# Long convolution and two MLPs on one core: sums move from GpSimd to VectorE, the filter's clamps are shared with ScalarE, the last rows go from SBUF to SBUF

## The chip, the cores and the metric

The kernel runs on one core of one Trainium2 chip. The metric is device time in microseconds (us): the median of the runs of one program. In this text PE is TensorE, PEld its weight loads, DVE is VectorE, ACT is ScalarE, POOL is GpSimd and SP is SyncE; ACTq and SPq are the DMA queues of ACT and SP.

## What is computed

```python
h_filt = (np.maximum(pos_emb @ w1, 0.0) @ w2) * np.exp(-0.01 * pos)[:, None]
u = x * v                                            # 12480 x 128
y = irfft(rfft(u, n=2 * S, axis=0) * rfft(h_filt, n=2 * S, axis=0), n=2 * S, axis=0)[:S]
a = x * y                                            # convolution, then the gate
b = np.maximum(a @ moe_w_in, 0.0) ** 2 @ moe_w_out        # 128 -> 2048 -> 128
g = b @ moe2_w_in
out = g * (1.0 / (1.0 + np.exp(-1.702 * g))) @ moe2_w_out # 128 -> 2048 -> 128
```

The MLP weights are 64-bit floats in memory; the kernel splits each into two 32-bit parts.

## The kernel before

The order of the work is written out by hand: each engine takes its instructions in the order in which the code issues them, and so do the two DMA queues. There are four stages.

**Filter stage** (`filter_stage`). Eight groups of eight columns j. For each, PE multiplies eight position tiles by `w1` (L256, `hp`), DVE clamps and windows the two halves of the result into `r` (L261, two instructions of 512 elements), and the sum and the difference of the halves go to `h`: the sum on POOL (L265; on DVE in the last group), the difference on DVE (L267). `spare` (L246) issues matmuls whose results nobody reads, 5 ahead of the stage and 13 behind it. A matmul of 32-bit floats shows as two records.

**First transform** (`s1_step`, L278, L282): the 16 steps of the filter `h`, then the 32 of the input `u`, into `G` and `A`.

**Second transform** (`stage_s2`): 99 frequencies, in 50 pairs p. Per pair PE makes `xk` (L348), now and then `fk` (L325) and `hk` (L340) for the filter, and with two pairs' delay the way back `ob` (L369). DVE multiplies (`t`, L357), and the two halves of the product are made on POOL (L360) and DVE (L361). ACT copies `ob` into `A` (L371; one PSUM buffer for `ob`), and every second pair the rows go to the DRAM tile `bd` (L378). `work.tick(p)` puts one step of the weights' conversion behind each pair's product: a chunk of 512 columns is eight DVE instructions (L135 to L148, L152) and one ACT cast (L150), one step to a tick; seven chunks start 6.5 pairs apart.

**Handover**. The last three rows go to `bd` (L374), then `load_first` (L458) reads rows 88 to 98 back into `A`, transposed; `work.finish()` completes two chunks; `sums_first` (L433) makes six sums on DVE; `front_y(0)` runs the inverse transform (L516, `yps`) of the first tile, `split_first` (L504 to L506) multiplies by x, and the MLP starts. `spare` (L645) issues 8 matmuls ahead of it and one behind it.

**MLP** (`mlp`). 25 tiles of 490 to 504 columns, each in 8 units per layer. `unit_in` (L560 to L562, L578, `hin`) is the first product of a unit with ACT's ReLU and square (L588, L589) or sigmoid (L593); `gate` and `low` (L601, L603, L612) make the two parts `gh` and `gl`; `unit_out` (`acc`) follows four units later. The first 40 units belong to layer 0; from then on layers 0 and 1 alternate. For the next tile `load_b` fetches 198 KB pieces `uv` from `bd` and POOL makes four sums `b` of 256 elements out of each (L433); `front_y` does the inverse transform and the product with x (L529; the columns that are left over, `yr`, on POOL, L532). Eight more weight chunks of 512 columns are converted, one step to a unit, started 6 units apart.

Of the kernel before, what the change touches and what calls it, by code (L numbers as in the profile page):

```python
# [1 line left out]

# [21 lines left out]
N1, N2 = 99, 127  # L24
# [7 lines left out]
NWC = DFF // WC  # L32
NP = -(-N1 // 2)
# [16 lines left out]
LAG = 4  # L50
SHIFT = 40
# [18 lines left out]
def widths():  # L70

    whole = [sum(s[3] for s in WHOLE[SPT * t:SPT * t + SPT]) for t in range(NTILE)]
    rest, left = [], RESTW
    for t, w in enumerate(whole):
        n = 0
        if t and left:
            n = min(left, -(-RESTW // (NTILE - 1)))
# [18 lines left out]
def conv_mlp_kernel(ctx: ExitStack, tc: tile.TileContext, xc, xt, vc, pt, w1, w2,  # L96
# [16 lines left out]
    def load_raw(n, pool):  # L113
        i, c = divmod(n, NWC)
        raw = pool.tile([128, WC, 2], I32, tag="raw", name="raw", bufs=2)
# [3 lines left out]
        else:  # L119
            k = WC // 128  # L120
# [4 lines left out]
    def conversion(n, raw, pool):  # L125

        i, c = divmod(n, NWC)
        cols = slice(c * WC, (c + 1) * WC)  # L130
        low, high = raw[:, :, 0], raw[:, :, 1]
        s = pool.tile([128, WC], I32, tag="cs", name="cs", bufs=2)
        hi, lo = (wts[i // 2][:, 2 * (i % 2) + k, cols] for k in range(2))
        vec = nc.vector
        yield vec.tensor_scalar(out=s, in0=high, scalar1=20, scalar2=0x7FF,  # L135
                                op0=ALU.logical_shift_right, op1=ALU.bitwise_and)
        yield vec.tensor_scalar(out=s, in0=s, scalar1=896.0, scalar2=1151.0, op0=ALU.max, op1=ALU.min)
        yield vec.tensor_scalar(out=s, in0=s, scalar1=896.0, scalar2=float(1 << 23),
                                op0=ALU.subtract, op1=ALU.mult)
        yield vec.scalar_tensor_tensor(out=s, in0=high, scalar=-(1 << 31), in1=s,  # L140
                                       op0=ALU.bitwise_and, op1=ALU.bitwise_or)
        m = pool.tile([128, WC], I32, tag="cm", name="cm", bufs=2)
        f = m.bitcast(FP32)
        yield vec.tensor_scalar(out=m, in0=high, scalar1=0xFFFFF, scalar2=0x100000,
                                op0=ALU.bitwise_and, op1=ALU.bitwise_or)
        yield vec.scalar_tensor_tensor(out=f, in0=low.bitcast(U32), scalar=2.0 ** -32, in1=m,
                                       op0=ALU.mult, op1=ALU.add)
# [11 lines left out]
    class Weights:  # L159
# [3 lines left out]
        def __init__(self, chunks, start, gap, lead, pool, rest=()):  # L163
            self.pool, self.raw, self.run = pool, {}, []
            self.plan = [(int(start + k * gap), n) for k, n in enumerate(chunks)]
            self.fetches = [(at - lead, n) for at, n in self.plan] + [(at, n) for at, n in rest]
            self.plan += [(1 << 30, n) for at, n in rest]

        def tick(self, i):
            self.run = [g for g in self.run if next(g, self) is not self]  # L170
            if self.fetches and self.fetches[0][0] <= i:
                n = self.fetches.pop(0)[1]
                self.raw[n] = load_raw(n, self.pool)
            if self.plan and self.plan[0][0] <= i and self.plan[0][1] in self.raw:
                n = self.plan.pop(0)[1]
                self.run.append(conversion(n, self.raw.pop(n), self.pool))
                next(self.run[-1])

        def finish(self):
            while self.run or self.plan:  # L180
                self.tick(1 << 30)

# [37 lines left out]
    def filter_stage(fp, bank, h, inputs):  # L220
# [4 lines left out]
        warm = fp.tile([128, 128], FP32, name="warm", bufs=1)  # L225
# [22 lines left out]
        spare(5, warm[:, 1:128], warm[:, 1:128])  # L248
        for j in range(0, NJ, JF):
            for c in range(j // HC + 12, min(j // HC + 12 + JF // HC, NC_)):  # L250
                load_pos(c)
            if j >= JF:
                inputs.load()
            ps = bank("hp")[:N1]
            for i in range(JF):
# [8 lines left out]
            last = j + JF == NJ  # L264
            (nc.vector if last else nc.gpsimd).tensor_tensor(  # L265
                out=h[:, :, j:j + JF], in0=r[:, 0], in1=r[:, 1], op=ALU.add)
            nc.vector.tensor_tensor(out=h[:, :, NJ + j:NJ + j + JF], in0=r[:, 0], in1=r[:, 1],  # L267
                                    op=ALU.subtract)
        spare(13, p_t[NC_ - 1][:, 0, :], bw1)
# [35 lines left out]
    def stage_s2(sp, mp, A, w2b, hooks, work):  # L305
# [9 lines left out]
        with kp as kp, obp as obp:  # L315
# [49 lines left out]
            def back(p):  # L365
                n, m, P = pair(p), m_t.pop(p), P_t.pop(p)
                ob = obp.tile([128, 2, 2, D], FP32, tag="ob", name="ob")
# [3 lines left out]
                nc.scalar.copy(out=A[:, 2 * p:2 * p + n], in_=ob[:, 0:n])  # L371
                if p == NP - 1:
                    for h, queue in ((0, nc.scalar), (1, nc.sync)):
                        queue.dma_start(out=bd[h, 0:JF1, k], in_=A[h * NJ:h * NJ + JF1, k])  # L374
# [6 lines left out]
            for p in range(NP + 2):  # L381
# [6 lines left out]
                elif p % 4 == 0:  # L388
                    filters(p // 2)
                    filters(p // 2 + 1)  # L390
                if 0 <= p - 2:
# [6 lines left out]
                if p < NP - 2:  # L398
# [7 lines left out]
    def tile_parts(segs):  # L406

        at = 0
# [7 lines left out]
    b_t, x_t = {}, {}  # L416
# [14 lines left out]
    def combine(k, s, c, engine):  # L431
        uv, b = b_t[k]
        engine.tensor_tensor(out=b[:, :, s, c], in0=uv[:, 0, :, c], in1=uv[:, 1, :, 1 - c],  # L433
                             op=ALU.add if s != c else ALU.subtract)

    def load_b(bp, t):


        last = max(p[0] for p in whole(t)) // JG
        for k in range(loaded[0], last + 1):  # L440
            uv = bp.tile([N1, 2, JG, 2, D], FP32, tag="uv", name="uv", bufs=2)
            for h in range(2):
                nc.sync.dma_start(out=uv[:, h], in_=bd[h, k * JG:(k + 1) * JG].rearrange("j k c d -> k j c d"))
            b = sums(bp, (k - 1) % 3)
            b_t[k] = uv, b
            for s in range(1 if k < KF else 2):
                for c in range(2):
                    combine(k, s, c, nc.gpsimd)
        loaded[0] = last + 1

    late_h = []

    def load_first(A, rows):


        for h in range(2):
            queue = nc.scalar if rows.stop == N1 and h else nc.sync
            queue.dma_start(out=A[rows, h * JF1:(h + 1) * JF1],  # L458
                            in_=bd[h, 0:JF1, rows].rearrange("j k c d -> k j c d"))
        for h, k in late_h:  # L460
            nc.sync.dma_start(out=bd[h, JF1:NJ, k], in_=A[h * NJ + JF1:(h + 1) * NJ, k])
# [387 lines left out]
```

## Time and profile before

| | |
|---|---|
| median of 3 runs (lowest, highest) | 1390.95 us (1390.25, 1391.91) |
| the profiled execution: its own time, its span | 1392.53 us, 1390.7 us |
| busy: PE, PEld | 1377.2 us (99%), 1143.1 us (82%) |
| busy: DVE, ACT, POOL | 1104.7 us (79%), 949.6 us (68%), 208.9 us (15%) |
| granted TensorE clock, mean | 0.998 |
| HBM read, written | 63.62 MB, 24.81 MB |

The profiled execution's own time is 1.83 us more than its span: what lies ahead of the first and behind the last instruction. Busy shares are of the whole span. The filter stage takes about the first 22 us, the transforms last until 227 us, the handover until 239 us, and the MLP takes the rest; what the change touches lies mostly at the seams, so it is read there and not in the shares.

### The profile page before, as it was taken

Reading aid. Unit: us, or ns where it says so; the run is one execution under the profiler, and the core shown is the slowest. Engines: PE = TensorE matmul, PEld = TensorE weight load, DVE = VectorE, ACT = ScalarE, POOL = GpSimd, SP = SyncE. Lnnn points to the kernel's source line nnn. Section 1 sums busy time; section 2 is a strip of 40 time slices with the busy share of each in tenths; the row PEclk is TensorE's granted clock in tenths of the full one; section 3 lists DMA queues with packets and bytes.
Section 4 is the critical chain, followed back from the end, with each engine's and each line's share of the span. In section 5 each row is a group of like instructions: output and inputs, shape, how many; then the busy total and the mean of one; then the engine's idle time right before and its main releaser. Section 6 shows DMA issues by size and latency. Waiting matters only on the chain.

```text
span 1390.7 us, 19236 instructions
## 1 busy us (share of the span) xinstructions
PE 1377.2 (99%) x7756; PEld 1143.1 (82%) x7756; DVE 1104.7 (79%) x1170; ACT 949.6 (68%) x1071; POOL 208.9 (15%) x208
## 2 busy tenths in 40 slices
PE   9999998999999999999999999999999999999998
PEld 8888885878788888888888888888888888888887
DVE  7559997888997777778777877777777777778887
ACT  2655553888776776667677776777677766777776
POOL 3013333522221011201121011111110120000000
PEclk9999999999999999999999999999999999999999
DMA  9967785212100001000010000100000100000000
GB/s 261 307 215 265 269 266 178 77 50 69 47 20 27 25 10 32 27 27 9 20 39 27 8 27 20 39 9 27 20 27 8 39 19 9 8 8 8 8 15 15
DMA packets 46583, 89.67 MB, mean 64 GB/s; under 512 B 4221, under 2 KB 31038, under 8 KB 45982
## 3 DMA queue, kind: packets, MB, share of 16 engines
q1 hardware_dynamic: 37427, 63.69, 15.1%
q10 hardware_dynamic: 9067, 24.75, 4.7%
q8 instruction: 61, 1.00, 0.3%
q14 instruction: 28, 0.23, 0.0%
HBM read 63.62 MB, written 24.81 MB: 64 GB/s over the span
## 4 chain that ended last, share of the span: by engine, by line
PE 79%; DVE 2%; ACT 2%; issue 0%; ACTq 0%
PE acc L560 13%; PE hin L560 13%; PE hin L561 13%; PE acc L561 13%; PE hin L562 12%; PE acc L562 12%; PE yps L516 3%; DVE gl L612 1%; ACT g L589 1%; ACT g L588 1%; DVE gh L601 0%; DVE g L603 0%; ACT gh L591 0%; DVE lo L493 0%; PE hin L578 0%
## 5 line engine op out<-in xcount | busy, mean ns | idle before, releaser
L612 DVE TENSOR_TENSOR gl<-g,gh 128x1004 fp32r<-128x1004 f32 (+4 forms) x400 | 493.6, 1234 | 33.8 <-ACT gh L608 33.6
L588 ACT ACTIVATE g<-hin 128x1004 f32<-128x1004 f32 (+4 forms) x200 | 201.1, 1005 | 226.9 <-PE hin L562 214.5
L560 PE MATMUL acc<-gh,w 128*128 128x502 f32 (+4 forms) x800 | 314.0, 392 | 2.4 <-DVE lo L493 2.4
L561 PE MATMUL acc<-gl,w 128*128 128x502 f32 (+4 forms) x800 | 312.1, 390 | 1.3 <-DVE gl L612 1.2
L562 PE MATMUL acc<-gh,w 128*128 128x502 f32 (+4 forms) x800 | 311.6, 390 | 0.0
L560 PE MATMUL hin<-hi,w 128*128 128x502 f32 (+4 forms) x798 | 311.3, 390 | 0.3 <-DVE g L603 0.3
L561 PE MATMUL hin<-lo,w 128*128 128x502 f32 (+4 forms) x798 | 311.0, 390 | 0.0
L562 PE MATMUL hin<-hi,w 128*128 128x502 f32 (+4 forms) x798 | 310.5, 389 | 0.0
L603 DVE TENSOR_TENSOR g<-hin,g 128x1004 f32<-128x1004 f32 (+4 forms) x200 | 238.6, 1193 | 46.6 <-ACT g L593 46.4
L601 DVE CAST gh<-g 128x1004 fp32r<-128x1004 f32 (+4 forms) x185 | 132.8, 718 | 152.0 <-ACT g L589 152.0
L593 ACT ACTIVATE g<-hin 128x1004 f32<-128x1004 f32 (+4 forms) x200 | 200.0, 1000 | 73.8 <-PE hin L562 65.8
L589 ACT ACTIVATE g<-g 128x1004 f32<-128x1004 f32 (+4 forms) x200 | 208.0, 1040 | 6.3
L608 ACT CAST gh<-g 128x1004 fp32r<-128x1004 f32 (+4 forms) x200 | 202.7, 1014 | 1.7 <-DVE g L603 1.7
L560 PEld LDWEIGHTS acc<-gh,w 128*128 128x128 f32 x800 | 150.9, 189 | 35.6 <-DVE lo L493 2.8
L560 PEld LDWEIGHTS hin<-hi,w 128*128 128x128 f32 x798 | 150.5, 189 | 34.8 <-ACT g L588 2.1
L561 PEld LDWEIGHTS acc<-gl,w 128*128 128x128 f32 x800 | 150.7, 188 | 31.9 <-DVE gl L612 2.5
L562 PEld LDWEIGHTS acc<-gh,w 128*128 128x128 f32 x800 | 150.7, 188 | 30.7
L562 PEld LDWEIGHTS hin<-hi,w 128*128 128x128 f32 x798 | 150.8, 189 | 30.4
L561 PEld LDWEIGHTS hin<-lo,w 128*128 128x128 f32 x798 | 150.9, 189 | 29.9
L433 POOL TENSOR_TENSOR Gs<-uv 99x256 f32<-99x256 f32 x82 | 91.8, 1149 | 442.2 <-DMA uv<-bd 367.2
L433 POOL TENSOR_TENSOR b<-uv 99x256 f32<-99x256 f32 x44 | 48.9, 1140 | 269.9 <-DMA uv<-bd 194.8
L360 POOL TENSOR_TENSOR P<-t 128x256 f32<-128x256 f32 (+1 forms) x50 | 48.1, 961 | 155.6 <-DVE t L357 139.2
(72 smaller groups left out, 1047.2 us busy)
## 6 DMA issues: line engine op xcount, KB each, us to landing
uv<-bd SPq DMA_DIRECT2D x64, 198.0 KB
m<-in_c_s_dram SPq DMA_DIRECT2D x49, 256.0 KB
bd<-A ACTq DMA_DIRECT2D x24, 512.0 KB
x<-in_xc_dram SPq DMA_DIRECT2D x16, 384.0 KB
v<-in_vc_dram SPq DMA_DIRECT2D x16, 384.0 KB
Gs<-gd ACTq DMA_DIRECT2D x10, 512.0 KB
raw<-in_moe_w_in_dram SPq DMA_DIRECT2D x8, 512.0 KB
raw<-in_moe_w_out_dram SPq DMA_DIRECT2D x8, 512.0 KB
```

What stands on the lines that cost most here:

```text
L360: nc.gpsimd.tensor_tensor(out=P[:, 0:n, 1], in0=t[:, 0:n, 0, 1], in1=t[:, 0:n, 1, 0], op=ALU.add)
L433: engine.tensor_tensor(out=b[:, :, s, c], in0=uv[:, 0, :, c], in1=uv[:, 1, :, 1 - c], op=ALU.add if s != c else ALU.subtract)
L560: nc.tensor.matmul(out=out, lhsT=a, rhs=hl[0], start=first, stop=False)
L561: nc.tensor.matmul(out=out, lhsT=a, rhs=hl[1], start=False, stop=False)
L562: nc.tensor.matmul(out=out, lhsT=b, rhs=hl[0], start=False, stop=last)
L588: nc.scalar.activation(out=g, in_=ps, func=ACTF.Relu)
L589: nc.scalar.activation(out=g, in_=g, func=ACTF.Square)
L593: nc.scalar.activation(out=g, in_=ps, func=ACTF.Sigmoid, scale=1.702)
L601: nc.vector.tensor_copy(out=gh, in_=g)
L603: nc.vector.tensor_tensor(out=g, in0=ps, in1=g, op=ALU.mult)
L608: nc.scalar.copy(out=gh, in_=g)
L612: nc.vector.tensor_tensor(out=gl, in0=g, in1=gh.bitcast(FP32), op=ALU.subtract)
```

## The change

- Filter stage: `r` is laid out column by column (j outside, f inside) with three buffers. ACT clamps half of the second half, a quarter of the layer, in four instructions of 64 elements each (L287), except in the last group, which is cut into two groups of four columns. The sum and the difference are therefore written to `h` with one element every 128 words. 7 spare matmuls stand ahead of the stage (5 before) and 6 behind it (13 before).
- Second transform: all eight layer-0 chunks are ticked there, started exactly 6 pairs apart, and the ticks end four pairs before the last instead of two; the last filter group is made two pairs earlier; the next to last `ob` takes another PSUM buffer, the last one is copied by DVE.
- Handover: rows 92 to 98 go straight from SBUF to SBUF, one row and half to a DMA (L402), rows 88 to 91 through `bd` as before. Three ticks of the conversion run ahead of the first sums, the rest of it behind the first tile's front. That front is cut in pieces with small spares between them.
- MLP: POOL's sums go to DVE, two instructions of 512 elements for a piece instead of four of 256, one of them issued ahead of each layer-0 gate (`combine_next`). Pieces are fetched a tile earlier. Layer 1's weights are converted in four chunks of 1024 columns, 12 units apart, in one shared tile `words`. The left-over columns' product goes to DVE, and left-over columns start in tile 2 instead of 1.

```diff
-            r = fp.tile([N1, 2, F, JF], FP32, tag="r", name="r")
-            for s in range(2):
-                wb = win[:, s, j:j + JF].unsqueeze(1).to_broadcast([N1, F, JF])
-                nc.vector.scalar_tensor_tensor(
-                    out=r[:, s], in0=ps.rearrange("p (j s f) -> p s f j", j=JF, s=2)[:, s],
-                    scalar=0.0, in1=wb, op0=ALU.max, op1=ALU.mult)
...
+            ps = ps.rearrange("p (j s f) -> p s j f", j=JF, s=2)
+            late = j + JF >= NJ
+            r = fp.tile([128, 2, JF, F], FP32, tag="r", name="r", bufs=3)[:N1]
+            for s, n in ((0, m), (1, m if late else HC)):
+                wb = win[:, s, j:j + n].unsqueeze(2).to_broadcast([N1, n, F])
+                nc.vector.scalar_tensor_tensor(out=r[:, s, 0:n], in0=ps[:, s, 0:n], scalar=0.0, in1=wb,
+                                               op0=ALU.max, op1=ALU.mult)
+            if not late:
+                for i in range(HC, m):
+                    nc.scalar.activation(out=r[:, 1, i], in_=ps[:, 1, i], func=ACTF.Relu,
+                                         scale=win[:, 1, j + i:j + i + 1])
+            for n, (engine, op) in enumerate(((nc.vector if late else nc.gpsimd, ALU.add),
+                                              (nc.vector, ALU.subtract))):
+                engine.tensor_tensor(out=h[:, :, n * NJ + j:n * NJ + j + m].rearrange("p f j -> p j f"),
+                                     in0=r[:, 0, 0:m], in1=r[:, 1, 0:m], op=op)
+        spare(6, p_t[NC_ - 1][:, 0, :], bw1)
...
+                ob = (kp.tile([128, FK, D], FP32, tag="fk", name="ob", bufs=1).rearrange(
+                    "p (k c) d -> p k c d", c=2) if p == NP - 2 else
+                      obp.tile([128, 2, 2, D], FP32, tag="ob", name="ob"))
...
+                (nc.vector.tensor_copy if p == NP - 1 else nc.scalar.copy)(
+                    out=A[:, 2 * p:2 * p + n], in_=ob[:, 0:n])
+                for i in range(2 * p, 2 * p + n):
+                    if i >= DIRECT:
+                        for h, queue in ((0, nc.scalar), (1, nc.sync)):
+                            queue.dma_start(out=A[i:i + 1, h * JF1:(h + 1) * JF1],
+                                            in_=A[h * NJ:h * NJ + JF1, i])
+                if p == NP - 4:
+                    load_first(A, slice(88, DIRECT))
...
-                if p < NP - 2:
+                if p < NP - 4:
                     work.tick(p)
...
+    def combine_two(uv, b, op):
+        b = b.rearrange("n j s c d -> n j (s c) d")
+        u, v = uv[:, 0], uv[:, 1]
+        if op == ALU.add:
+            nc.vector.tensor_tensor(out=b[:, :, 1:3], in0=u[:, :, ::-1], in1=v, op=op)
+        else:
+            nc.vector.tensor_tensor(out=b[:, :, 0:4:3], in0=u, in1=v[:, :, ::-1], op=op)
+    def combine_next(n):
+        for i in range(min(n, len(pending))):
+            pending.pop(0)()
...
+            for a, b, n in ((0, 2, 2), (2, 3, 4), (3, SPT, 0)):
+                at = inverse(ps, whole(0)[a:b], at)
+                if n:
+                    spare(n, 128)
...
-        spare(8)
+        spare(4)
         front_y(0)
         spare(1)
-        load_rest()
+        load_b(bp, 1)
+        combine_next(2)
+        work.finish()
         prev = None
-        work = Weights([8, 12, 9, 13, 10, 14, 11, 15], 3, 6, 3, cp)
+        work = Weights([(2, 0), (3, 0), (2, 1), (3, 1)], 6, 12, 4)
...
+                if l == 0:
+                    combine_next(1)
                 gate(un)
...
-            work = Weights([0, 4, 1, 5, 2, 6, 3], 3, 6.5, 5, cp, [(46, 7)])
+            work = Weights([(i, c) for c in range(NWC) for i in range(2)], 3, 6, 5)
...
-            load_first(A, slice(88, N1))
-            work.finish()
+            store_late(A)
+            work.finish(EARLY)
             sums_first(bp, A)
```

`DIRECT` is 92, `EARLY` 3 and `NP` 50. `store_late` writes the last row's columns to `bd` on SP.

**DVE, filter stage, one group and the last one.** `r<-hp` are the clamps, `h<-r` the difference (and, in the last group, the sum). Before:

```order
L261 SCALAR_TENSOR_TENSOR r<-hp,win 99x512 x2
L267 TENSOR_TENSOR h<-r 99x64x8
L261 SCALAR_TENSOR_TENSOR r<-hp,win 99x512 x2
L265 TENSOR_TENSOR h<-r 99x64x8
L267 TENSOR_TENSOR h<-r 99x64x8
```

Now:

```order
L283 SCALAR_TENSOR_TENSOR r<-hp,win 99x512
L283 SCALAR_TENSOR_TENSOR r<-hp,win 99x256
L291 TENSOR_TENSOR h<-r 99x8x64
L283 SCALAR_TENSOR_TENSOR r<-hp,win 99x256 x2
L291 TENSOR_TENSOR h<-r 99x4x64 x2
L283 SCALAR_TENSOR_TENSOR r<-hp,win 99x256 x2
L291 TENSOR_TENSOR h<-r 99x4x64 x2
```

One clamp of each group is half as long, the result is written with f inside, and the last group has two of everything.

**DVE, from the last products to the first sums** (`t` and `P` are the product of a pair, `cs`, `cm`, `words` and `w` the conversion, `Gs<-A` the six first sums). Before:

```order
L357 TENSOR_TENSOR t<-xk,hc 128x512
L361 TENSOR_TENSOR P<-t 128x128
L148 SCALAR_TENSOR_TENSOR cm<-cm,cs 128x512
L135 TENSOR_SCALAR cs<-raw 128x512
L137 TENSOR_SCALAR cs<-cs 128x512
L138 TENSOR_SCALAR cs<-cs 128x512
L152 TENSOR_TENSOR w_958<-cm,w_958 128x512
L140 SCALAR_TENSOR_TENSOR cs<-raw,cs 128x512
L144 TENSOR_SCALAR cm<-raw 128x512
L146 SCALAR_TENSOR_TENSOR cm<-raw,cm 128x512
L433 TENSOR_TENSOR Gs<-A 99x2x128 x6
```

(of which `L148` and `L152` come once more ahead of `L433`). Now:

```order
L381 TENSOR_TENSOR t<-xk,hc 128x512
L385 TENSOR_TENSOR P<-t 128x128
L397 COPY A<-ob 128x256
L153 SCALAR_TENSOR_TENSOR words<-words 128x512
L157 TENSOR_SCALAR words<-words 128x512
L171 TENSOR_TENSOR w_987<-words,w_987 128x512
L159 TENSOR_SCALAR words<-words 128x512
L465 TENSOR_TENSOR Gs<-A 99x2x128 x6
```

Ten conversion instructions stood there, four are left, and the copy of the last row is new; the others follow the first tile's front.

**ACT, at the same place, now** (`A<-A` are row DMAs, `w_987<-words` the last two casts of the conversion, `g` the first units' ReLU and square):

```order
L397 COPY A<-ob 128x512
L402 DMA A<-A 1x4x256 x3
L169 CAST w_987<-words 128x512 x2
L653 ACTIVATE g<-hin 128x2x492
L654 ACTIVATE g<-g 128x2x492
```

The second cast stands ahead of the first unit's ReLU; before, both casts were ahead of the first sums.

## Rows read from the trace of the kernel before

**Rows 1.** The page's first part: busy us, share of the span, instructions.
```profile
PE 1377.2 (99%) x7756; PEld 1143.1 (82%) x7756; DVE 1104.7 (79%) x1170; ACT 949.6 (68%) x1071; POOL 208.9 (15%) x208
```
**Rows 2.** Waits of PE, whole span: us in total, times, longest.
```profile
PE acc L560 <- DVE lo L493: 2.4, 1, 2.4
...
PE acc L561 <- DVE gl L612: 1.2, 2, 0.7
```
**Rows 3.** Three stretches: length, busy PE, PEld, DVE, ACT, POOL, clock, DMA share, GB/s.
```profile
160.00:200.00 40.00, 40.00 (x295) 34.78 (x295) 38.44 (x48) 20.20 (x32) 13.65 (x15) 1.00 0.81 267
230.00:243.00 13.00, 11.10 (x63) 6.45 (x62) 8.17 (x15) 1.84 (x3) 4.44 (x6) 0.87 0.63 193
350.00:400.00 50.00, 47.60 (x234) 38.74 (x232) 45.46 (x55) 33.88 (x37) 14.01 (x12) 0.97 0.15 46
```
**Rows 4.** Timeline, filter stage: start, us, instruction, [idle before it, releaser].
```profile
6.88 1.29 DVE L261 SCALAR_TENSOR_TENSOR r<-hp,win 99x512 f32<-99x512 f32 x2 [5.88 <-PE hp L256]
8.20 0.69 DVE L267 TENSOR_TENSOR h<-r 99x512 f32<-99x512 f32 x1
8.81 1.28 DVE L261 SCALAR_TENSOR_TENSOR r<-hp,win 99x512 f32<-99x512 f32 x2
...
18.95 3.00 PE L246 MATMUL spare<-bw,pos 128*99 128x128 f32 x26
...
21.68 0.69 DVE L265 TENSOR_TENSOR h<-r 99x512 f32<-99x512 f32 x1
...
22.52 22.00 PE L278 MATMUL s<-cs,h 99*64 99x198 f32 x255 [0.57 <-DVE h L265]
```
**Rows 5.** The tile r: duration ns min/median/max of POOL's additions.
```profile
L265 POOL TENSOR_TENSOR h<-r x7: 1773/1780/1785, 8.2 to 19.8; 99x512 f32<-99x512 f32 x7
```
**Rows 6.** Timeline, three of the last products of the second transform.
```profile
217.69 1.21 DVE L357 TENSOR_TENSOR t<-xk,hc 128x1024 f32<-128x1024 f32 x1
...
220.49 1.21 DVE L357 TENSOR_TENSOR t<-xk,hc 128x1024 f32<-128x1024 f32 x1
...
222.15 1.22 DVE L357 TENSOR_TENSOR t<-xk,hc 128x1024 f32<-128x1024 f32 x1
```
**Rows 7.** Timeline, handover.
```profile
227.05 6.76 PE L645 MATMUL spare<-xs,ci 99*99 99x492 f32 x16
...
227.65 0.27 ACTq L374 DMA_DIRECT2D bd<-A  x1
...
229.34 0.35 ACTq L458 DMA_DIRECT2D A<-bd  x1
...
233.50 0.62 ACT L150 CAST w<-cm 128x512 fp32r<-128x512 f32 x1 [3.15 <-DVE cm L148]
...
234.76 2.62 DVE L433 TENSOR_TENSOR Gs<-A 99x256 f32<-99x256 f32 x6
...
239.16 2.49 PE L578 MATMUL hin<-hi,w 128*128 128x492 f32 x4
...
242.13 0.99 ACT L588 ACTIVATE g<-hin 128x984 f32<-128x984 f32 x1 [8.01 <-PE hin L578]
```
**Rows 8.** Chain of waits, start of the MLP: start, us, what.
```profile
244.78 0.83 PE yps L516 x16
...
249.20 0.42 PE acc L560
```
**Rows 9.** Timeline, MLP: a conversion step alone, POOL's sums, the step beside them.
```profile
351.49 0.68 DVE L140 SCALAR_TENSOR_TENSOR cs<-raw,cs 128x512 int32<-128x512 int32 x1
...
368.49 2.35 POOL L433 TENSOR_TENSOR Gs<-uv 99x256 f32<-99x256 f32 x2
...
369.00 1.24 DVE L140 SCALAR_TENSOR_TENSOR cs<-raw,cs 128x512 int32<-128x512 int32 x1
```
**Rows 10.** Timeline, the second piece uv: its DMAs, and sums waiting for it.
```profile
234.14 5.95 SPq L443 DMA_DIRECT2D uv<-bd  x4
...
241.46 1.46 POOL L433 TENSOR_TENSOR Gs<-uv 99x256 f32<-99x256 f32 x2 [2.12 <-DMA uv<-bd]
```

More of the change, by code (lines that the diff above doesn't have):

```diff
@@ L1 @@
 from contextlib import ExitStack
+from functools import partial
 import numpy as np
@@ L50 @@
 LAG = 4
+EARLY = 3
+DIRECT = 92
 SHIFT = 40
@@ L75, in widths @@
         n = 0
-        if t and left:
-            n = min(left, -(-RESTW // (NTILE - 1)))
+        if t > 1 and left:
+            n = min(left, -(-RESTW // (NTILE - 2)))
             n += (w + n) % 2
@@ L111, in conv_mlp_kernel, with words, load_raw @@
     wts = []
-    def load_raw(n, pool):
-        i, c = divmod(n, NWC)
-        raw = pool.tile([128, WC, 2], I32, tag="raw", name="raw", bufs=2)
+    space = []
+    def words(at, n):
+        return space[0][:, at * WC:(at + n) * WC]
+    def load_raw(n, m):
+        i, c = n
+        w = WC2 if i > 1 else WC
+        raw = words(2 * (m % 2) * (i < 2), 2 * w // WC).rearrange("p (a b) -> p a b", b=2)
         if i % 2 == 0:
@@ L123, in load_raw, with conversion @@
         return raw
-    def conversion(n, raw, pool):
-        i, c = divmod(n, NWC)
-        cols = slice(c * WC, (c + 1) * WC)
+    def conversion(n, m, raw):
+        i, c = n
+        w = raw.shape[1]
         low, high = raw[:, :, 0], raw[:, :, 1]
-        s = pool.tile([128, WC], I32, tag="cs", name="cs", bufs=2)
-        hi, lo = (wts[i // 2][:, 2 * (i % 2) + k, cols] for k in range(2))
+        hi, lo = (wts[i // 2][:, 2 * (i % 2) + k, c * w:(c + 1) * w] for k in range(2))
         vec = nc.vector
[L135 to L142, printed above, removed]
-        f = m.bitcast(FP32)
[L144 to L147, printed above, removed]
@@ L159, in conv_mlp_kernel, with __init__ @@
     class Weights:
[L163 to L167, printed above, removed]
+        def __init__(self, chunks, start, gap, lead):
+            self.raw, self.run = {}, []
+            self.plan = [(start + k * gap, k, n) for k, n in enumerate(chunks)]
+            self.fetches = [(at - lead, k, n) for at, k, n in self.plan]
         def tick(self, i):
@@ L171, in tick, with finish @@
             if self.fetches and self.fetches[0][0] <= i:
[L172 to L176, printed above, removed]
+                _, k, n = self.fetches.pop(0)
+                self.raw[n] = load_raw(n, k)
+            if self.plan and self.plan[0][0] <= i and self.plan[0][2] in self.raw:
+                _, k, n = self.plan.pop(0)
+                self.run.append(conversion(n, k, self.raw.pop(n)))
                 next(self.run[-1])
-        def finish(self):
-            while self.run or self.plan:
+        def finish(self, n=1 << 30):
+            while n and (self.run or self.plan):
                 self.tick(1 << 30)
+                n -= 1
     class Inputs:
@@ L436, in load_b, with pend, load_uv @@
+    def pend(k):
+        pending.extend(partial(combine_two, *b_t[k], op) for op in (ALU.add, ALU.subtract))
+    def combine_next(n):
+        for i in range(min(n, len(pending))):
+            pending.pop(0)()
+    def load_uv(bp, k):
+        uv = bp.tile([N1, 2, JG, 2, D], FP32, tag="uv", name="uv", bufs=2)
+        for h in range(2):
+            nc.sync.dma_start(out=uv[:, h], in_=bd[h, k * JG:(k + 1) * JG].rearrange("j k c d -> k j c d"))
+        return uv
     def load_b(bp, t):
         last = max(p[0] for p in whole(t)) // JG
+        for k, s in again:
+            uv = load_uv(bp, k)
+            for c in range(2):
+                pending.append(partial(combine, uv, b_t[k][1], s, c))
+        again.clear()
@@ L440, in load_b @@
         for k in range(loaded[0], last + 1):
[L441 to L444, printed above, removed]
+            uv = load_uv(bp, k)
+            b = sums(bp, k % 3)
             b_t[k] = uv, b
-            for s in range(1 if k < KF else 2):
-                for c in range(2):
-                    combine(k, s, c, nc.gpsimd)
+            pend(k)
@@ L449, in load_b @@
         loaded[0] = last + 1
-    late_h = []
+    late_h, again = [], []
     def load_first(A, rows):
         for h in range(2):
-            queue = nc.scalar if rows.stop == N1 and h else nc.sync
-            queue.dma_start(out=A[rows, h * JF1:(h + 1) * JF1],
-                            in_=bd[h, 0:JF1, rows].rearrange("j k c d -> k j c d"))
+            nc.sync.dma_start(out=A[rows, h * JF1:(h + 1) * JF1],
+                              in_=bd[h, 0:JF1, rows].rearrange("j k c d -> k j c d"))
@@ L539, in load_rest @@
             assert all(p[0] // JG == k for p in REST)
-            uv = bp.tile([N1, 2, JG, 2, D], FP32, tag="uv", name="uv", bufs=2)
-            for h in range(2):
-                nc.sync.dma_start(out=uv[:, h], in_=bd[h, k * JG:(k + 1) * JG].rearrange("j k c d -> k j c d"))
-            b = sums(bp, 2)
+            uv = load_uv(bp, k)
+            b = words(6, 2)[0:N1].bitcast(FP32).rearrange("p (j s c d) -> p j s c d", j=JG, s=2, c=2)
             b_t[k] = uv, b
-            for s in range(2):
-                for c in range(2):
-                    combine(k, s, c, nc.gpsimd)
+            pend(k)
         def front_rest():
@@ L675, in mlp @@
                         front_y(t + 1)
+                    if j == 4 + late and t + 2 < NTILE:
+                        load_b(bp, t + 2)
                     if j == 5 + late and t + 1 < NTILE:
```

113 lines of the change are left out of this document (68 added, 45 removed).

## The prediction

> **What bounds the kernel now.** The page's first part comes first: PE is busy for 1377.2 us of a span of 1390.7 us [rows 1]. So 13.5 us are PE's to lose, and a faster DVE, ACT or POOL is worth only what it takes off them or off a lowered clock. The change leaves PE's columns as they are (left-over columns move by a tile), so only the seams can move the time. The list of PE's waits tells where two of them are: 2.4 us on `lo` and 1.2 us on `gl`, both in the MLP [rows 2]. The windows give the clock: 0.97 in 350 to 400 us, 0.87 in 230 to 243 us [rows 3]. The timeline shows the other seams: the end of the filter stage, where PE's first transform waits for the last sum [rows 4], and the handover, where PE is kept going by matmuls that nobody reads [rows 7]. Those count as busy, so a seam costs more than PE's idle time there. The chain of waits goes through the first units of the MLP [rows 8].
>
> The sum is made against the profiled execution, which took 1392.53 us by its own time over a span of 1390.7 us [rows 1]; the median of the runs is 1390.95 us (1390.25 to 1391.91), 1.6 us lower. I take the difference of the parts off the median. A measurement of this kernel can tell about 0.2%, 2.8 us, from no change: faster is below 1388.2 us, slower above 1393.7 us.
>
> **A. Filter stage: −0.5 us.** A group now starts 8.81 − 6.88 = 1.93 us after the one before it: two clamps, 1.29 us, and a difference, 0.69 us [rows 4]. With a quarter of the clamps on ACT, DVE has 1.5 × 0.64 + 0.69 = 1.65 us. But POOL's sum takes 1.78 us [rows 5], and it shares its time with DVE's difference of two SBUF operands, as a conversion step shows that takes 0.68 us alone and 1.24 us beside POOL [rows 9]. So about 1.78 us a group is what three buffers can reach: 7 × 0.15 = 1.0 us saved. The last group, all on DVE, becomes eight instructions of half the size; at some 0.36 us each (half of 0.64 to 0.69 us, and a fixed part) that is 2.9 us where 1.29 + 2 × 0.69 = 2.7 us stood. It starts earlier, on its first half. I take 0.5 us off the start of the first transform, 22.52 us [rows 4]. The six spares last 6/13 of 3.00 us, 1.4 us, so PE will idle near 2 us ahead of the transform; whether the clock falls then is in the range. Bounds: −1.5 us, if POOL hides too, and, above, the rival below on the writes.
>
> One thing there no row shows: `h` is now written with a hop of 128 words at every element, where runs of eight words stood, at 0.69 us for 512 elements [rows 4]. I keep 0.69 us, the nearest row, and twice that as the upper end. [...]
>
> **B. Second transform: −1.0 us.** DVE is already busy for 38.44 of 40 us there [rows 3], and the ticked chunks come every 6 pairs, not 6.5, which puts up to some 4 us of conversion more into the body; little more than 4 us of DVE's idle time lie there to take it (1.56 us in each 40). I count +1.4 us for what doesn't fit. Against that the last two ticks go from between the last products: two of those stand 2.80 us apart with conversion between them and 1.66 us without [rows 6], so 2 × 1.1 = 2.2 us less at the end, and the second PSUM buffer for `ob` saves part of one copy's wait (about 0.2 us). Together −1.0 us; bounds −3 and +3, by either part alone and the clock.
>
> **C. Last rows to first sums: −4.5 us.** Now the last `ob` ends at 227.05 us, where the spares start, and the first sums start at 234.76 us: 7.7 us [rows 7], through two DRAM trips and the end of two chunks' conversion. Afterwards: the copy, 0.6 us (the nearest is the cast of the same size, 0.62 us), three row DMAs' issue on ACT's queue, 3 × 0.27 us, and a landing of 1.7 us, as the store at 227.65 was followed by its reader's issue at 229.34 us [rows 7]: 3.1 us. DVE's four steps fit beside that, about 4 × 0.65 = 2.6 us. I take 3.2 us, so −4.5, and the sums start near 234.76 − 5.5 = 229.3 us. The four spares, half of 6.76 us [rows 7], cover 3.4 us of it. Bounds: −6 us (a landing in 0.3 us) and 0 (the row DMAs queue behind the stores on ACT's queue).
>
> **D. First sums to the steady MLP: +1.4 us.** Now 249.20 − 234.76 = 14.4 us, with 0.83 us of the left-over columns' transform in it [rows 8], which moves to later work. Behind the first sums, `hin` starts 4.4 us on and ACT's first ReLU ends 242.13 + 0.99 − 234.76 = 8.4 us on [rows 7]. Afterwards DVE, done with the front at about +5.5 us, still has two sums and three conversion steps (to +8.1), and ACT's second cast, 0.6 us [rows 7], stands ahead of the first ReLU: it ends at about +9.7 us. PE has two PSUM buffers for `hin`, 2.49 us of work [rows 7], and then idles about 2.5 us. I take 1.3 us for the later ReLU, 0.9 us of clock (half of 13.00 × 0.13 = 1.7 us, what the present stretch lost [rows 3]), and −0.83 us: +1.4 us. Bounds −0.8 us (the cast is out of the way) and +3 us.
>
> **E. MLP: −4.5 us.** The waits on `lo` and `gl` [rows 2] and the clock of 0.97 over 50 us, 1.5 us [rows 3], are 5.1 us. Beside them POOL's sums run, and a DVE step beside a POOL sum takes 1.24 us for 0.68 us [rows 9]. Without POOL nothing holds DVE. What comes instead is 62 sums of 512 elements, some 62 × 0.69 [rows 4] = 43 us, in front of the gates; DVE is busy 79% [rows 1], so 286 us are free, and the product of a unit follows four units after its first part. I keep 0.6 us of waits. Bounds −5.1 us and 0.
>
> **At nothing:** the left-over columns' product on DVE and the chunks of 1024 columns (as many elements, four times eight instructions of twice the length) lie in DVE's idle time; if it is gone, each costs its own 1.3 us at a gate. The two early spares, 0.46 us at 3.00/13 us each [rows 4], lie ahead of the first group, while PE waits for its input.
>
> **Sum:** −0.5 − 1.0 − 4.5 + 1.4 − 4.5 = −9.1; 1390.95 − 9.1 = **1382 us**.
>
> **The rivals.**
> *Writes of `h`.* If a hop at every element doubles a write, the difference takes 1.38 us and POOL's sum gets longer, about 2.4 us a group for 1.93 us: 7 × 0.47 + 0.8 for the last group = 4 us, in place of −0.5, and PE idles long enough to lose the clock, up to 1.7 us as in 230 to 243 us [rows 3]; less with part of it. 1382 + 4.5 + 1 = 1387.5 us. For it: DVE's write is the only port whose pattern changes. Against it: reads of every second word (`raw`) take the ordinary 0.68 us [rows 9]. Chance 0.22.
> *The handover's gain is eaten.* The row DMAs land 2 us later, behind the store on the same queue, or the cast ahead of the ReLU costs the whole clock: +4 us, 1386 us. Chance 0.11.
> *The sums do as much in front of the gate on DVE as on POOL.* E is 0: 1386.5 us. For it: the waits name DVE's tiles, not POOL [rows 2]. Against it: the held step [rows 9]. Chance 0.09.
> *Slower: the sums stand in DVE's queue and wait for their piece.* At present POOL alone waits for `uv`; its DMAs took 5.95 us from 234.14 us, and POOL waited 2.12 us [rows 10]. Afterwards a late piece holds the gate, and everything behind it on DVE. It decides where a piece lands later than its gate by more than the four units by which the second product trails. At 1 us in each of 23 tiles, with 4.5 us of E lost on top: 1382 + 23 + 4.5 = 1409 us, or about 1396 us if half of the tiles are hit and E holds. Against it: pieces are fetched a tile earlier, (1390.7 − 239) / 25 = 46 us. Chance 0.06.
>
> **How the numbers follow.** The forecast has 0.52, with its own range 1378 to 1385 us. The three rivals at 1386 to 1387.5 us have 0.42, the slower one 0.06. The range 1377.5 to 1389.5 us takes in the forecast's bounds and the three. Same, 1388.2 to 1393.7 us, is the upper part of the first three rivals and of a forecast that fails in B, 0.12; slower 0.07, the last rival and a little of the first two together; faster 0.81.
>
> **What would show it.** A: the difference (L291) at 0.69 us and the transform (L302) at 22.0 us; at 1 us or more the first rival holds. B and C: the first sums (L465) at 229.3 us. D: PE idle after two units, with ReLU (L653) at +9.7 us from the sums and a clock of 0.85 to 0.95 there. E: POOL silent after the second transform, a clock of 1.00 in 350 to 400 us, and no wait over 0.6 us on `lo` or `gl`. A wait of DVE on `uv`, or PE busy for much more than 1377.2 us less 4 us of spares, would make the prediction wrong.

## The result and the profile after

The changed kernel takes 1400.97 us (1400.74 to 1402.26) against 1391.43 us (1390.25 to 1392.46) for the kernel before in runs beside it: 1.0076 times as long, 95% interval 1.0064 to 1.0088. I had forecast 1382 us and a range up to 1389.5 us. The change is 9.5 us slower, and the prediction has the wrong sign. The traced execution of the kernel before took 1392.53 us, 1.1 us above this median, so the marks of the two traces below end 8.2 us apart.

The first part of the page after, which answers to [rows 1]:

```profile
PE 1379.2 (99%) x7750; PEld 1150.5 (82%) x7750; DVE 1110.7 (79%) x1229; ACT 955.3 (68%) x1094; POOL 62.5 (4%) x61
```

PE is still 99% busy, of a span of 1399.0 us. Its busy time grew by 2 us, though nine spare matmuls fewer stand at the old places; a PE at half clock counts as busy here all the same (8.00 of 8 us in 244 to 252 us, at a clock of 0.50). PE's waits, whole span after (us in total, times, longest), answer to [rows 2]:

```profile
PE s L302 <- DVE h L291: 4.3, 1, 4.3
PE yps L584 <- DVE Gs L465: 3.7, 1, 3.7
PE hp L276 <- ACT r L287: 2.3, 2, 1.9
PE spare L266 <- ACT r L287: 1.9, 1, 1.9
...
PE hin L625 <- ACT g L653: 1.0, 2, 0.6
PE acc L625 <- DVE lo L552: 0.6, 1, 0.6
PE acc L626 <- DVE gl L677: 0.5, 1, 0.5
```

The two stalls in the MLP are down from 3.6 to 1.1 us. In their place stand 8.5 us in the filter stage (on `h` and on ACT's `r`) and 3.7 us ahead of the first sums. Four stretches after, in the columns of [rows 3]:

```profile
20.00:50.00 30.00, 23.49 (x225) 21.46 (x227) 26.34 (x37) 12.43 (x34) 6.04 (x3) 0.77 0.83 209
240.00:250.00 10.00, 6.33 (x47) 5.19 (x48) 3.60 (x9) 0.62 (x1) 0.00 (x0) 0.68 0.51 146
250.00:260.00 10.00, 9.03 (x38) 5.85 (x34) 7.66 (x13) 4.95 (x6) 0.00 (x0) 0.81 0.42 150
350.00:400.00 50.00, 49.40 (x280) 40.54 (x279) 44.71 (x52) 39.02 (x42) 0.00 (x0) 1.00 0.16 48
```

The clock is 1.00 in 350 to 400 us, where it was 0.97. Against that, 0.77 over 30 us comes from some 14 us at 0.50, half clock: from about 21.6 us, inside the filter stage, where PE waits 1.9 us for ACT for the second time, to about 35 us, some 5 us into the first transform (the clock is 0.70 in 20 to 24 us, 0.50 from there to 34 us, 0.68 in 34 to 36 us). In the handover 0.68 and 0.81 come from some 10 us at half clock (0.50 from 244 to 252 us, 0.88 and 0.56 in the 2 us ahead and behind).

Where the time went, by starts and ends in the two traces (us):

| mark | before | after | after − before | change since the mark above |
|---|---|---|---|---|
| first transform starts | 22.52 | 30.51 | +7.99 | +7.99 |
| first transform's last matmul ends | 87.56 | 97.56 | +10.00 | +2.01 |
| last `ob` ends | 227.21 | 236.79 | +9.58 | −0.42 |
| first sums start | 234.76 | 243.28 | +8.52 | −1.06 |
| first `acc` matmul | 249.13 | 261.85 | +12.72 | +4.20 |
| 401st `acc` matmul | 448.92 | 456.62 | +7.70 | −5.02 |
| last `acc` matmul ends | 1387.13 | 1395.34 | +8.21 | +0.51 |

The filter stage (with the clock it leaves behind) costs 10.0 us, the way into the MLP 4.2 us, and the MLP gives back 4.5 us (5.0 us up to the 401st `acc`). The timeline of the filter stage after, groups one and two and the end, answers to [rows 4] and [rows 5]:

```profile
6.33 1.02 DVE L283 SCALAR_TENSOR_TENSOR r<-hp,win 99x512 f32<-99x512 f32 x2 [5.34 <-PE hp L276]
7.44 0.93 ACT L287 ACTIVATE r<-hp,win 99x64 f32<-99x64 f32 x4 [4.11 <-DVE r L283]
8.40 1.06 DVE L291 TENSOR_TENSOR h<-r 99x512 f32<-99x512 f32 x1 [1.05 <-ACT r L287]
8.45 2.03 POOL L291 TENSOR_TENSOR h<-r 99x512 f32<-99x512 f32 x1 [8.01 <-ACT r L287]
9.30 1.01 DVE L283 SCALAR_TENSOR_TENSOR r<-hp,win 99x512 f32<-99x512 f32 x2
...
23.28 2.88 PE L266 MATMUL spare<-bw,pos 128*99 128x128 f32 x12 [1.85 <-ACT r L287]
...
30.51 3.91 PE L302 MATMUL s<-cs,h 99*64 99x198 f32 x21 [4.35 <-DVE h L291]
```

ACT doesn't clamp beside DVE. It waits until DVE's clamps of the same group are done (the releaser is `DVE r`), and DVE, whose next instruction is the difference, waits for ACT. The three steps of a group follow one another, 9.30 − 6.33 = 2.97 us, where a group took 1.93 us.

The handover after, in the timeline:

```profile
234.05 1.49 SPq L402 DMA_DIRECT2D A<-A  x2
...
236.63 3.46 PE L712 MATMUL spare<-xs,ci 99*99 99x492 f32 x8
...
237.79 0.58 ACT L397 COPY A<-ob 128x512 f32<-128x512 f32 x1 [1.77 <-DMA A<-A]
237.95 3.66 SPq L402 DMA_DIRECT2D A<-A  x5
238.41 1.88 ACTq L402 DMA_DIRECT2D A<-A  x3
...
243.28 2.10 DVE L465 TENSOR_TENSOR Gs<-A 99x256 f32<-99x256 f32 x6 [1.27 <-DMA A<-A]
...
247.24 2.03 PE L712 MATMUL spare<-xs,ci 99*99 99x128 f32 x8
...
251.71 2.40 PE L643 MATMUL hin<-hi,w 128*128 128x492 f32 x4
```

A row DMA takes 0.60 to 0.75 us of its queue (1.49 us for two on SP, 1.88 us for three and 1.20 us for two on ACT), not the 0.27 us of [rows 7]. Seven stand on each queue, on SP among the loads through DRAM (L512), and on ACT the copy of the next `ob` stands behind them. The sums start 2.2 us after SP began to issue its last row DMA (5 from 237.95 us, the last about 241.0 us). PE idles 3.7 us ahead of the first tile's front, which then runs at half clock (0.50): `hin` starts 8.4 us behind the sums, where it was 4.4 us [rows 7].

### The profile page after: what moved, and what is told of

It is laid out like the page before. It is cut to its first block, busy times and chain, and to the rows that moved or that the text cites. A ratio compares the mean times of both kernels' runs of the same rounds, so it can differ in the third digit from the quotient of the medians.

```text
span 1399.0 us, 19106 instructions
## 1 busy us (share of the span) xinstructions
PE 1379.2 (99%) x7750; PEld 1150.5 (82%) x7750; DVE 1110.7 (79%) x1229; ACT 955.3 (68%) x1094; POOL 62.5 (4%) x61
## 4 chain that ended last, share of the span: by engine, by line
PE 96%; DVE 2%; ACT 1%; issue 1%; DMA 0%; ACTq 0%; SPq 0%; DVEq 0%
PE acc L625 13%; PE acc L626 13%; PE acc L627 13%; PE hin L626 13%; PE hin L625 13%; PE hin L627 13%; PE s L302 5%; PE yps L584 4%; PE xk L372 3%; PE ob L395 3%; PE hk L364 2%; PE fk L349 1%; PE hp L276 1%; DVE r L283 0%; DVE t L381 0%
## 5 line engine op out<-in xcount | busy, mean ns | idle before, releaser
L677 DVE TENSOR_TENSOR gl<-g,gh 128x1004 fp32r<-128x1004 f32 (+4 forms) x400 | 477.2, 1193 | 36.9 <-ACT gh L673 36.8
L666 DVE CAST gh<-g 128x1004 fp32r<-128x1004 f32 (+4 forms) x185 | 125.8, 680 | 136.5 <-ACT g L654 136.5
L381 DVE TENSOR_TENSOR t<-xk,hc 128x1024 f32<-128x1024 f32 (+1 forms) x50 | 60.1, 1202 | 10.5 <-ACT hc L366 10.5
L395 PE MATMUL ob<-P,m 128*128 128x256 f32 x198 | 53.1, 391 | 0.3 <-issue 0.3
```

What stands on the lines that cost most here:

```text
L395: nc.tensor.matmul(out=ob[:, j], lhsT=m[:, j, 1, :], rhs=P[:, j])
L666: nc.vector.tensor_copy(out=gh, in_=g)
L677: nc.vector.tensor_tensor(out=gl, in0=g, in1=gh.bitcast(FP32), op=ALU.subtract)
```

## The experiments

All stand on the changed kernel. The two runs with a PSUM tile for ACT and spare8 keep the changed filter stage or a variant of it; in front_kept and all runs described after it the filter stage is that of the kernel before, so that the handover and the MLP are seen without its 10 us.

**The filter stage back (filter_before).** The function `filter_stage` is that of the kernel before, spares and all; nothing else is touched.

> The changed kernel with the filter stage of the kernel before. By the trace after, the stage's end moved from 22.52 to 30.51 us, and the first transform lost 2.0 us more at half clock: the theory that the stage carries the loss expects the transform back at 22.5 us, no half clock up to 240 us, and 1401 - 10 = 1391 us. A rival, that most of it is given back later because the weights' conversion and the second transform are bound by DVE, expects 1394 us or more.

Measured: 1390.27 us (1388.67 to 1390.86), 0.9992 times before, interval 0.9983 to 1.0001. The transform starts at 22.72 us:

```profile
22.72 3.58 PE L297 MATMUL s<-cs,h 99*64 99x198 f32 x36 [0.61 <-DVE h L284]
```

The stage carries the whole loss; the rest of the change is worth nothing that this measurement tells from zero. The expectation of no half clock up to 240 us failed: the handover's half clock, behind 230 us, is still there (0.80 over 226 to 260 us, below).

**A PSUM tile for ACT's columns (own_bank, own_bank_runs).** ACT takes columns 6 and 7 of each group, both halves, from a second PSUM tile: as many elements as before, in as many instructions.

```diff
+            own = m if j + JF >= NJ else 6
             ps = bank("hp")[:N1]
+            pa = bank("hp")[:N1] if own < m else None
             for i in range(m):
-                nc.tensor.matmul(out=ps[:, i * 2 * F:(i + 1) * 2 * F],
+                to, k = (ps, i) if i < own else (pa, i - own)
+                nc.tensor.matmul(out=to[:, k * 2 * F:(k + 1) * 2 * F],
...
-                    nc.scalar.activation(out=r[:, 1, i], in_=ps[:, 1, i], func=ACTF.Relu,
+                    nc.scalar.activation(out=r[:, s, i], in_=pa[:, s, i - own], func=ACTF.Relu,
```

The second run lays `r` out with f outside again, so that `h` is written in runs of eight words:

```diff
-            r = fp.tile([128, 2, JF, F], FP32, tag="r", name="r", bufs=3)[:N1]
+            r = fp.tile([128, 2, F, JF], FP32, tag="r", name="r", bufs=3)[:N1]
```

> The changed kernel, but ScalarE's quarter of a group is two whole columns in a PSUM tile of their own, so that VectorE and ScalarE read different PSUM tiles; the hopping writes to h stay. Theory 1 (the two engines take turns at one PSUM tile, and the difference stands in VectorE's queue behind ScalarE's four clamps: 1.02 + 0.93 + 1.06 = 2.97 us a group) expects ScalarE beside VectorE's clamps, 1.0 + 1.06 = 2.06 us a group, the transform at about 24 us and 1393 to 1395 us. Theory 2 (the hopping writes alone are the loss) expects nearly the old 2.97 us a group and over 1399 us.

> As the one with a PSUM tile of its own, and r is laid out as before (f outside, the columns inside), so that h is written in runs of eight words. If the hop is what makes the difference 1.06 us and POOL's sum 2.03 us, they go back to 0.69 and 1.78 us; a group then takes 1.78 us, the transform starts at about 21.5 us, and the time is 1390 to 1391.5 us. If the writes do not matter, the difference stays near 1.06 us and the time within 0.5 us of the run with hopping writes.

Measured: 1393.77 us (1391.95 to 1395.33) and 1391.12 us (1390.56 to 1393.45). The timeline of the first, two groups and the transform:

```profile
6.38 1.02 DVE L288 SCALAR_TENSOR_TENSOR r<-hp,win 99x384 f32<-99x384 f32 x2 [5.38 <-PE hp L279]
6.82 0.93 ACT L291 ACTIVATE r<-hp,win 99x64 f32<-99x64 f32 x4 [3.48 <-PE hp L279]
7.78 1.06 DVE L295 TENSOR_TENSOR h<-r 99x512 f32<-99x512 f32 x1 [0.38 <-ACT r L291]
7.83 14.07 POOL L295 TENSOR_TENSOR h<-r 99x512 f32<-99x512 f32 x7 [7.38 <-ACT r L291]
...
9.79 1.06 DVE L295 TENSOR_TENSOR h<-r 99x512 f32<-99x512 f32 x1
...
24.13 2.07 PE L306 MATMUL s<-cs,h 99*64 99x198 f32 x20 [2.74 <-DVE h L295]
```

ACT now starts beside DVE's clamps, released by PE, and a group takes 9.79 − 7.78 = 2.01 us. Both engines still write the same `r`, so what made them take turns was the PSUM tile that both read. The timeline of the second:

```profile
8.32 0.69 DVE L295 TENSOR_TENSOR h<-r 99x512 f32<-99x512 f32 x1 [0.43 <-ACT r L291]
8.37 12.32 POOL L295 TENSOR_TENSOR h<-r 99x512 f32<-99x512 f32 x7 [7.93 <-ACT r L291]
...
10.07 0.69 DVE L295 TENSOR_TENSOR h<-r 99x512 f32<-99x512 f32 x1
...
22.58 3.84 PE L306 MATMUL s<-cs,h 99*64 99x198 f32 x26 [1.78 <-DVE h L295]
```

With runs of eight words the difference is back at 0.69 us, and POOL's seven sums take 12.32 us instead of 14.07 us. The hop costs 0.37 us a difference; it is the smaller part of the loss (2.7 us between the two medians, where the tile of its own took 7.2 us off the change). The transform starts at 22.58 us, where I had expected 21.5 us: groups follow at 1.75 us, but the first difference comes no earlier (8.32 us for 8.20 us in [rows 4]). In this execution PE's first ten matmuls and not six, as in own_bank, take 0.42 us instead of 0.27 us, so the clamps start 0.48 us later than there (6.86 us for 6.38 us), and then the difference waits 0.43 us for ACT. The last two half groups take 3.3 us (19.46 to 22.76 us). PE then idles 1.8 us behind six spares, and the clock falls, to a mean of 0.83:

```profile
20.00:30.00 10.00, 8.22 (x76) 7.96 (x76) 9.83 (x16) 2.64 (x6) 0.68 (x1) 0.83 1.01 254
```

The first transform takes 66.46 us for 64.88 us in own_bank, 1.6 us more. This traced execution took 1393.05 us, 1.9 us above the median of its kernel, so some of that may be its own. As built here, the sharing without turns gains nothing over the old stage (1390.27 us). No run tries it with thirteen spares behind it, or with the next group's clamps ahead of the difference.

**Eight spares (spare8).** One line: `spare(8)` for `spare(4)` ahead of `front_y(0)`.

> The changed kernel with eight spare matmuls ahead of the first tile's front instead of four, as before the change. PE idles 3.7 us there now and runs at half clock for 10.2 us behind it. If that clock makes the first tile's front longer (8.4 us from the sums to the first unit, 4.4 before), eight spares keep the clock up and give about 4 us back: 1397 us. The rival, that the front is bound by VectorE and by its inputs' landing, expects 1400 us or more.

Measured: 1399.26 us (1398.04 to 1401.19), 1.7 us less than the change, where 4 us were expected; the two ranges overlap, so the gain itself is not clear of noise. `hin` does start 5.07 us behind the sums, not 8.43 us; but PE is then stopped two units further on (timeline):

```profile
245.31 2.10 DVE L465 TENSOR_TENSOR Gs<-A 99x256 f32<-99x256 f32 x6 [1.33 <-DMA A<-A]
...
250.38 1.34 PE L643 MATMUL hin<-hi,w 128*128 128x492 f32 x4
...
254.46 0.62 ACT L169 CAST w<-words 128x512 fp32r<-128x512 f32 x1 [11.55 <-DVE words L167]
254.99 0.98 ACT L653 ACTIVATE g<-hin 128x984 f32<-128x984 f32 x1
...
256.02 0.72 PE L625 MATMUL hin<-hi,w 128*128 128x492 f32 x1 [2.40 <-ACT g L653]
```

This is the wait that part D named: the cast of the conversion stands ahead of the first ReLU, both PSUM buffers of `hin` are full, and PE idles 2.4 us. The ReLU ends 10.7 us behind the sums (forecast 9.7 us), and the clock falls there instead: it is 1.00 in 240 to 256 us and 0.57 in 256 to 260 us, where PE's matmuls of 492 columns take 0.61 us instead of 0.38 us. In the change itself the late front hid most of it (0.63 us of wait at the same place).

**Spares and cast together (front_kept), the cast alone (steps_early).** `EARLY = 7` for 3 puts four more conversion steps, the second cast among them, ahead of the first sums; `front_kept` has `spare(8)` as well.

> The changed kernel with the filter stage of the kernel before (1390.3 us), eight spare matmuls ahead of the first tile's front, and four more steps of the conversion (EARLY 7, the second cast among them) ahead of the first sums, where VectorE waits for the rows. Theory: PE's idle 3.4 us there, and the 2.4 us that PE waited for the first ReLU behind the cast in the run with eight spares, each bring on a lowered clock. With both gone I expect the first unit's ReLU about 8.5 us behind the sums, no clock of 0.5 between 226 and 260 us, and 1385 to 1387 us. Rival: the rows' landing sets the time, spares or not, and the sums start later behind the four steps: 1389 us or more.

> The changed kernel with the filter stage of the kernel before (1390.3 us) and the four more conversion steps ahead of the first sums, but with four spares only. Theory (the lowered clock in the first tile's front costs more than the cast's place): PE idles some 4.3 us ahead of the sums, the clock falls as before, the cast is out of the way, and the time is 1389 to 1391 us, far from the 1385.8 us with eight spares. Rival (the cast's place was the main loss): 1387 us or less.

Measured: 1385.78 us (1385.29 to 1386.60), 0.9963 times before, interval 0.9950 to 0.9975; and, as expected, near filter_before: 1391.14 us (1390.01 to 1391.97). The same stretch in windows, filter_before and then front_kept:

```profile
226.00:260.00 34.00, 30.24 (x167) 22.22 (x167) 19.67 (x35) 16.14 (x19) 0.00 (x0) 0.80 0.41 128
```

```profile
226.00:260.00 34.00, 32.73 (x194) 23.21 (x195) 23.89 (x40) 19.87 (x22) 0.00 (x0) 1.00 0.44 138
```

Either cure alone gives 1.7 us at most (spare8 against the change; steps_early is 0.9 us above filter_before): in each of the two runs the idle stretch that is left was enough to bring the clock down (2.4 us in spare8, to 0.57 in 256 to 260 us; 4.2 us in steps_early, to 0.74 in 230 to 250 us). Together they take 4.5 us off filter_before.

**The row DMAs (rows_six, loads_behind, rows_six_kept).** In the first only rows 96 to 98 go from SBUF to SBUF, and rows 88 to 95 are read back from DRAM behind them. In the second all 14 row DMAs stay, and the loads of rows 88 to 91 stand behind them. The third is rows_six with the two cures of front_kept.

```diff
-DIRECT = 92
+DIRECT = 96
...
-                if p == NP - 4:
-                    load_first(A, slice(88, DIRECT))
                 if p == NP - 1:
+                    load_first(A, slice(88, DIRECT))
```

> The changed kernel with the filter stage of the kernel before (1390.3 us), and only rows 96 to 98 go from SBUF to SBUF (6 row DMAs instead of 14); rows 88 to 95 come back through DRAM behind them. Theory (the row DMAs hold each other up: 0.6 us of queue time each, and each waits for the eighth DMA before it): the sums start 1.5 to 2.5 us earlier than the 6.4 us behind the end of the products, 1388 to 1389 us. Rival (the landing of about 2 us sets it, and the trip through DRAM is no shorter): the sums start no earlier, 1390 us or more.

> The changed kernel with the filter stage of the kernel before (1390.3 us); all 14 row DMAs stay, but the four loads of rows 88 to 91 stand behind them in SP's queue, not between them. Theory (the row DMAs are late because they wait in SP's queue behind loads that wait for a store, and for DMAs that were issued eight before): the last row DMA is issued near 229.5 us instead of 230.4, the first sums start 0.5 to 1.2 us earlier than 232.7, and the time is 1388.5 to 1390 us. Rival (landing of the last one, or the load through DRAM, sets it): sums no earlier than 232.5 us, 1390 us or more.

> The faster version (filter stage of before, eight spares, four more steps ahead of the sums: 1385.8 us), and only rows 96 to 98 from SBUF to SBUF. The rows are then there some 0.5 us earlier, but VectorE's conversion steps end at about 233.6 us and PE's spares at 233.2 us: I expect the same within 0.7 us, 1385 to 1386.5 us.

Measured: 1388.67 us (1387.84 to 1391.64), 1390.82 us (1390.17 to 1391.59) and 1384.89 us (1384.29 to 1385.18). The SP queue and the sums in rows_six, and then in loads_behind:

```profile
226.85 2.23 SPq L397 DMA_DIRECT2D A<-A  x3
...
229.18 0.99 SPq L506 DMA_DIRECT2D A<-bd  x2
...
232.25 2.10 DVE L459 TENSOR_TENSOR Gs<-A 99x256 f32<-99x256 f32 x6 [1.65 <-DMA A<-bd]
```

```profile
226.08 3.56 SPq L397 DMA_DIRECT2D A<-A  x5
...
229.74 1.19 SPq L506 DMA_DIRECT2D A<-bd  x2
...
233.04 2.10 DVE L459 TENSOR_TENSOR Gs<-A 99x256 f32<-99x256 f32 x6 [1.35 <-DMA A<-bd]
```

With six row DMAs the sums start 5.8 us behind the start of the spares instead of 6.4 us: 0.6 us earlier, less than the 1.5 to 2.5 us that I expected, for now the loads through DRAM are last, and the sums start 2.1 us behind the end of their issue. That the time lies in the expected range all the same is luck; its interval, 0.9976 to 0.9995 times before, overlaps that of filter_before. In loads_behind the loads are late by the row DMAs ahead of them, and the sums start after 7.0 us: that expectation failed, and its rival held. rows_six_kept is 0.9 us below front_kept, a little more than the 0.7 us that I had allowed. What sets the end is the DMAs on SP's queue, 0.6 to 0.75 us for a row DMA and 0.5 to 0.6 us for a load, and about 2 us behind the last; changing the order moves the delay to others. That a DMA also waits for the eighth one before it, as I had put it, shows at the start of the trace before: the ninth DMA of the two queues together, a load of `pos`, waits 0.8 us for the first, of `bw`, to land. What that costs the row DMAs no run here separates, and it is left open. The trace after shows that SP's row DMAs do wait for earlier DMAs: 0.5 us for a store to `bd` and 0.3 us for a load from it.

**The sums back on POOL (pool_sums).** In `combine_two` `nc.gpsimd` stands for `nc.vector`.

> The changed kernel with the filter stage of the kernel before (1390.3 us), and the MLP's sums of pieces are made on GpSimd again, two instructions of 512 elements each as they stand in the queue now. Theory (POOL's sums held VectorE's steps, and the MLP's stalls went with them): stalls of some us come back on lo or gl, with a lowered clock around 370 us: 1393 to 1395 us. Rival (the earlier fetch and the wider conversion chunks took the stalls away, not the engine): within 1 us of 1390.3 us.

Measured: 1397.94 us (1397.65 to 1398.23), 7.7 us more than filter_before, where 3 to 5 us were expected. PE's waits are back:

```profile
PE acc L621 <- DVE gl L672: 3.9, 5, 1.3
...
PE hin L620 <- ACT g L648: 2.0, 2, 1.7
```

A stretch with four of POOL's sums, 390 to 410 us, in pool_sums and then in filter_before:

```profile
390.00:410.00 20.00, 18.32 (x108) 14.70 (x105) 19.38 (x18) 12.99 (x14) 7.47 (x4) 1.00 0.11 34
```

```profile
390.00:410.00 20.00, 20.00 (x90) 16.54 (x90) 17.67 (x19) 14.10 (x16) 0.00 (x0) 1.00 0.11 34
```

Beside POOL DVE is busy 19.38 of 20 us and PE loses 1.7 us; without it PE is busy throughout, with the same fetches and the same chunks. Part E's reason holds; as the sums stand now, in instructions of 512 elements, POOL costs even more than the 5.1 us that part E reads for the kernel before. It costs this only where DVE has little idle time: from the first to the 401st `acc` matmul pool_sums takes 200.7 us and filter_before 194.7 us, but from there to the last one 938.6 and 938.7 us, and in 450 to 900 us PE is busy throughout in both.

## Why the prediction was wrong, by its steps

**A, −0.5 us, was +10.0 us: this step made the sign wrong.** "With a quarter of the clamps on ACT, DVE has 1.5 × 0.64 + 0.69 = 1.65 us" took for granted that ACT works beside DVE and that DVE's difference finds ACT's part ready. Neither held. The two engines read the one PSUM tile in turns, and the difference stands in DVE's queue behind the wait: 1.02 + 0.93 + 1.06 = 3.01 us, and 2.97 us from group to group. Seven groups make 7 × 1.04 = 7.3 us of the 8.0 us; the half clock that follows PE's waits in the stage is the other 2.0 us. A PSUM tile of its own took 0.96 us off a group, and runs of eight words another 0.26 us. The trace after has ACT's start 0.09 us behind the end of DVE's second clamp, though that clamp reads only columns 0 to 3 of the tile, its first 512 words, and ACT only columns 4 to 7, the other 512. What the runs show is turns by the tile.

**The rival on the writes of `h`** had the right place and the wrong mechanism. The hop was priced between 0.69 and 1.38 us and measured 1.06 us; the rival's 4 us would have needed the upper end. The hop is worth 1.55 us (24.13 − 22.58 us) at the start of the transform in the two traces, and 2.7 us between the medians.

**B, −1.0 us, was −0.4 us** (−1.0 us in filter_before): within its bounds.

**C, −4.5 us, was −1.1 us.** The term mis-sized was the issue of a row DMA, "3 × 0.27 us", taken from a store to DRAM; it measured 0.60 to 0.75 us. I also counted three of them, where the copies on ACT and the loads on SP stand in one queue with seven, and I took the landing as 1.7 us where it was 2.2 us (1.9 us in filter_before). The rival "the handover's gain is eaten" named this place with 0.11.

**D, +1.4 us, was +4.2 us.** The ReLU behind the cast was right, and spare8 shows it. What I missed is that C's failure makes the four spares too short: I had taken "cover 3.4 us of it" for a sum start at 229.3 us, 3.2 us behind the last product; it came after 6.5 us, and the front then ran at half clock. Of the 4.0 us by which `hin` starts later behind the sums, spare8 shows 3.4 us to be that clock; the other 0.7 us are the front's new pieces and small spares, which the sum left out. With both cures (front_kept) the way from the sums to the first `acc` takes 13.4 us, 1.0 us less than before.

**E, −4.5 us, was −4.5 us,** from +12.72 to +8.21 us; pool_sums shows the reason. That the number is met exactly is in part luck. D counted the 0.83 us of the left-over columns' transform as gone, but it only moved: after, it stands at 278.15 us, behind the first `acc`, so E had to bear it, and the waits and the clock gave back about 5.3 us. The slower rival, sums waiting in DVE's queue for their piece, did not happen: from the 401st `acc` matmul to the end, some 18 tiles, the time grew by 0.51 us, where that rival had 1 us a tile, and the `acc` matmuls ahead of that mark have 780 columns fewer than before, which now follow it. (The 1396 us given for half of the tiles hit is wrong as a sum: 1382 + 11.5 is 1393.5 us.)

With A aside, filter_before came out at −1.2 us to before, where the rest of the sum promised −8.6 us: C and D cost 6.2 us of that. The other 1.2 us or so come from the base of the sum: its parts were read in an execution of 1392.53 us and taken off a median 1.6 us lower, and by the spans of the traces filter_before is 2.4 us shorter than before (1388.4 and 1390.7 us). The intended gain was there, and idle stretches of PE with the lowered clock behind them held it back: rows_six_kept, with the old filter stage, two numbers changed and eight row DMAs fewer, takes 1384.89 us, 0.9955 times before (interval 0.9939 to 0.9972), and is faster than both kernels.

## What to carry to other kernels

Before work is shared between two engines, look at what both read and at what stands next in the first one's queue: here two readers of one PSUM tile took turns (ACT 0.09 us behind DVE), and the in-order queue then added their times instead of overlapping them (1.02 + 0.93 + 1.06 us a group). Count every DMA on the queue that issues it, at its own measured issue time (here 0.60 to 0.75 us for a row DMA), with the work queued behind it, and add one landing at the end (here 2.2 us). At a seam where PE idles, price the clock with the wait, and remove every idle stretch there together, since here one of 2.4 us was enough to lose most of the gain.

## What had not been expected of the hardware

A DMA from SBUF to a single row of SBUF (4 KB) held the issuing queue for 0.60 to 0.75 us, where the store of the last rows to DRAM in the kernel before (12 KB) took 0.27 us [rows 7], although the row DMA moves less. What sets this price no run separates. And POOL paid for the hopping writes too, 2.03 us for 1.78 us a sum, a smaller share than DVE's 1.06 for 0.69 us.
